# Batch 0's second feed-forward product by plain matmuls in two passes, with its weights converted in their own place

## The chip, the cores and the metric

The kernel runs on one core of one Trainium2 chip. The metric is device time in microseconds (us); a time of the kernel is the median of its runs. The five engines are named as the profile names them: PE (TensorE matmul; PEld is its weight load), DVE (VectorE), ACT (ScalarE), POOL (GpSimd) and SP (SyncE, which here only issues transfers). [...]

## The reference

Two blocks follow each other. A hash attention gives `x`; a Fourier mixing block works on it. Cut to what matters:

```python
# q, k, v: (4 batches, 8 heads, 768, 64) float32; buckets from the signs of q@proj, k@proj
scores = where(q_bucket == k_bucket, scale * q @ k.T, -1e9)
x = softmax(scores) @ v                      # (4, 768, 512)
u = x + real(fft(fft(x, axis=1), axis=2))
un = (u - mean(u)) / sqrt(var(u) + 1e-6)     # per row
out = u + relu(un @ w_ch1) @ w_ch2           # (512, 2048) and (2048, 512)
```

The two weights arrive as 64-bit floats, so the kernel has to turn them into float32 itself. The change concerns the second product, `relu(...) @ w_ch2`, for the first of the four batches, and the way in which both weights come in.

## The kernel before

**Batches and stages.** The kernel goes through four batches. The attention of batch b+1 (24 steps, two heads at a time) is interleaved with the mixing of batch b. The mixing generator `mix(b)` yields after small pieces, and the main loop takes pieces from it in proportion to the attention's steps. The last batch's mixing has no attention beside it. In the first attention PE, DVE, ACT and POOL keep the written order; after it a scheduler places the instructions of every engine from the written order and its own estimates.

**The mixing** has these stages: folds and the two Fourier products (L1062, L1091), a transposition of `x` into six row tiles `u` (`across`, L1117), then for each of two halves of the 2048 hidden columns the first feed-forward product (`inner`, L1373 to L1421) and the second (`outer7`, L1221). Batch 0 therefore runs four such stages: first inner, first outer, second inner, second outer.

**Seven products for eight.** Both feed-forward products use a Strassen-like scheme (Winograd's): each matrix is cut into quarters, seven products of quarters replace eight, and sums of quarters are needed on both sides. In `outer7` a product is four matmuls of 128 x 128 weights against 256 columns, summed in one PSUM tile; three pairs of row tiles, seven products each, make 84 matmuls a half. The sums on the left side are DVE additions (`tile_sums` L1231 and L1232, L1266, L1274). The results are put together by ACT copies (L1265, L1276, L1279) and DVE additions (L1258, L1292, L1294, L1298). PSUM tiles of this stage come from a pool of two (`ps`, L521) while attention runs.

**The right side.** `right7` is seven tiles of 512 KB laid over `w2`: the quarters B11, B21, B22 and the sums T4, T1, T2, T3 for one half. For batch 0 the generator `weights2` (L1189) makes them: a row block of `w_ch2` (128 x 512, 64-bit, 512 KB) is fetched by POOL into one of two raw buffers (`zraw2`), `convert` writes its two column halves into two tiles of `right7`, and after every second block four DVE subtractions (L1212 to L1215) make the sums. Eight blocks make a half. Each half is stored to DRAM (`bd`, L1217), from where later batches fetch it (L1251). As the second half is written into the same seven tiles, its conversion can't begin before the first outer stage has read them; it runs during the second inner stage.

**A conversion** (`narrow`, L620) is DVE L631, L635 and an addition (L641 for one piece, L644 twice for two), ACT L639, L646 and L647. Only after L647 is the raw buffer free for the next fetch. The first weights (`weights1`, L703) go the same way, 16 blocks over seven raw buffers; the first seven fetches are issued by SP, the other nine by POOL (L685).

**The scratch tile `tq`** has six slots of 128 x 256. In batch 0 its first four hold the sums of quarters of the first weights for the inner stage (`quarters`, L1157, DVE L1164 to L1167, stored by SP L1170), one set for each of the eight hidden blocks; in an outer stage its slots are `temps`, for partial results.

**SP's queue** carries, in one order, the loads of q, k and v (L556, L562, L570), the stores of quarters (`ad`, L1169, L1170; `bd`, L1217), the ring of first-weight quarters for later batches (L1339) and the fetches of `right7` (L1251). POOL issues the output stores of batches 0 to 2 (L1000).

Of the kernel before, what the change touches and what calls it, by code (L numbers as in the profile page):

```python
# [20 lines left out]
P = 128  # L21
B, H, S, D = 4, 8, 768, 64
NBITS = 6
DM = H * D
# [455 lines left out]
def _main(  # L480
# [139 lines left out]
    def narrow(dst, raw, col, low=None):  # L620


        lo, hi = (raw[..., i] for i in range(2))
# [16 lines left out]
        if len(di.shape) == 2:  # L640
            nc.vector.tensor_tensor(di, di, low, op=ALU.add)  # L641
        else:
            for i in range(di.shape[1]):
                nc.vector.tensor_tensor(di[:, i], di[:, i], low[:, i], op=ALU.add)  # L644
# [27 lines left out]
    class Arrival:  # L672


        def __init__(self, slices, raws, col):
            self.slices, self.raws, self.col = slices, raws, col
            self.wide = slices[0][1].dtype == I64
            self.depth = len(raws) if self.wide else 4

        def fetch(self, i, queue):  # L680
            if i < len(self.slices):
                dst, src = self.slices[i]
                if self.wide:
                    raw = self.raws[i % self.depth].bitcast(I32)
                    queue.dma_start(raw.bitcast(I64), src)  # L685
                else:
                    n = dst.shape[-1]
                    queue.dma_start(
                        dst, src if len(dst.shape) == 2 else src.rearrange("p (s n) -> p s n", n=n)
                    )  # L690

        def convert(self, i, low=None):
            if self.wide:
                dst = self.slices[i][0]
                raw = self.raws[i % self.depth].bitcast(I32)
                if len(dst.shape) == 2:
                    raw = raw.rearrange("p (n w) -> p n w", w=2)
                else:
                    raw = raw.rearrange("p (s n w) -> p s n w", w=2, n=dst.shape[-1])
                narrow(dst, raw, self.col + i, low)  # L700
            self.fetch(i + self.depth, nc.gpsimd)

    def weights1():  # L703
# [10 lines left out]
        arrival = Arrival(slices, raws, 0)  # L714
        for i in range(arrival.depth):
            arrival.fetch(i, nc.sync)
# [472 lines left out]
    def weights2():  # L1189

        slices = []
        for half in range(2):
            for r in range(HF // 2):
                for hi, first in ((0, B11), (1, B21)):
                    c = half * HF // 2 + r + hi * HF

                    step = 1 if hi else T1 - B11
                    dst = w2f[:, 0 : 7 * QB].rearrange("p (i r n) -> p i r n", i=7, n=HD)
                    slices.append(
                        (dst[:, first : first + step + 1 : step, r],  # L1200
                         moe_w_ch2[c * P : (c + 1) * P, :])
                    )
        arrival = Arrival(slices, [zt2[:, i] for i in range(2)], NDC * DFF // WC)
        for half in range(2):
            for i in range(arrival.depth) if half == 0 else ():
                arrival.fetch(i, nc.gpsimd)
            for i in range(HF):
                arrival.convert(half * HF + i)
                yield
                if i % 2:  # L1210
                    b11, b21, b22, t4, t1, t2, t3 = (q[:, i // 2] for q in right7)
                    nc.vector.tensor_tensor(t3, b22, t1, op=ALU.subtract)  # L1212
                    nc.vector.tensor_tensor(t1, t1, b11, op=ALU.subtract)
                    nc.vector.tensor_tensor(t2, b22, t1, op=ALU.subtract)
                    nc.vector.tensor_tensor(t4, b21, t2, op=ALU.subtract)  # L1215
            for i in range(7):
                nc.sync.dma_start(bd[half, i], right7[i])  # L1217
            if half == 0:
                yield
# [350 lines left out]
```

## Time and profile before

| what | value |
|---|---|
| median of 10 runs | 1106.98 us (1104.31 to 1110.42) |
| the profiled execution's own time | 1106.58 us |
| its span, first to last instruction | 1104.8 us |
| PE busy in the span | 1049.5 us (95%) |
| DVE busy | 790.3 us (72%) |
| ACT busy | 499.6 us (45%) |
| POOL busy | 63.1 us (6%) |
| batch 0: first inner stage (first to last matmul of L1366) | 195.9 to 247.1 us |
| batch 0: first outer stage (L1246) | 262.0 to 306.7 us |
| batch 0: second inner stage | 306.9 to 369.1 us |
| batch 0: second outer stage | 369.7 to 413.2 us |

Busy time is the time in which an engine has an instruction under way. Matmuls overlap each other in the pipeline, so PE's busy time is a union, and a single matmul's duration is longer than its distance to the next one. Every float32 matmul appears as two records in the trace: the 84 matmuls of an outer half are 168 records.

### The profile page before, as it was taken

To read this page: it belongs to the slowest core of one execution; us is meant where nothing else is said; L and a number is where in the kernel's file an instruction comes from. 1 tells how busy PE (TensorE), PEld (TensorE's weight loads), DVE (VectorE), ACT (ScalarE), POOL (GpSimd) and SP (SyncE) were. 2 spreads that over 40 slices of the span, in tenths; PEclk is the share of its full clock that TensorE was granted. 3 is DMA by queue.
4 is the path that set the end of the run, shared out by engine and by line. 5 is a ranking of instruction groups with operands and counts; after the bars stand their busy time and mean duration, and the time that the engine had idled before them with its cause. 6 is when DMAs were issued, how large, how long until landed. Compare 5 with 4: busy or idle time off the path is not lost.

```text
span 1104.8 us, 14065 instructions
## 1 busy us (share of the span) xinstructions
PE 1049.5 (95%) x4893; PEld 636.5 (58%) x4893; DVE 790.3 (72%) x1326; ACT 499.6 (45%) x1055; POOL 63.1 (6%) x141
## 2 busy tenths in 40 slices
PE   6989888999999999999999999999999999999996
PEld 3333354445744675555664576645674569768675
DVE  5789968979598977786758785975856785744353
ACT  5879455654267324354425424354315532340420
POOL 0000000002000020010000011001000002100000
PEclk9999998999999999999999999999999999999998
DMA  8744434261046262323144134213032205122401
GB/s 223 202 100 106 92 106 109 93 201 26 20 126 182 79 185 60 60 60 76 26 152 107 51 67 167 43 35 94 20 109 83 68 29 172 53 82 83 127 20 42
DMA packets 175567, 103.13 MB, mean 93 GB/s; under 512 B 129408, under 2 KB 162816, under 8 KB 175488
## 3 DMA queue, kind: packets, MB, share of 16 engines
q1 hardware_dynamic: 168400, 83.93, 28.6%
q0 software_dynamic: 5520, 17.83, 5.2%
q8 instruction: 41, 0.67, 0.2%
q10 hardware_dynamic: 1568, 0.39, 0.2%
q14 instruction: 38, 0.31, 0.1%
HBM read 81.14 MB, written 20.97 MB: 92 GB/s over the span
## 4 chain that ended last, share of the span: by engine, by line
PE 56%; DVE 8%; ACT 3%; issue 1%; DMA 1%; DVEq 0%; ACTq 0%
PE o L1246 20%; PE h_p L1366 19%; PE oo L890 6%; PE sc L869 5%; PE cs L1062 2%; DVE pk L879 2%; PE A L1091 2%; PE B L1091 1%; DVE acc L964 1%; ACT rr L924 1%; DMA zraw<-in_moe_w_ch_dram 1%; DVE w L1258 1%; PE un L1117 1%; PE bits L804 1%; DVE h L1232 1%
## 5 line engine op out<-in xcount | busy, mean ns | idle before, releaser
L1246 PE MATMUL o<-w,h 128*128 128x256 f32 x1152 | 259.4, 382 | 1.1 <-ACT tq L1265 0.7
L1246 PEld LDWEIGHTS o<-w,h 128*128 128x128 f32 x1152 | 216.3, 190 | 43.5 <-issue 4.6
L873 ACT ACTIVATE pk<-sc 128x768 f32<-128x768 f32 x192 | 147.9, 809 | 82.8 <-PE sc L869 64.1
L1366 PE MATMUL h_p<-x,w 128*128 128x384 f32 x448 | 163.1, 494 | 3.8 <-ACT h L1388 2.3
L890 PE MATMUL oo<-pk,vn 128*64 128x385 f32 (+1 forms) x768 | 157.7, 505 | 3.6 <-DVE pk L879 3.0
L869 PE MATMUL sc<-qt,kt 64*128 64x384 f32 x768 | 153.8, 503 | 3.9 <-ACT pk L873 3.6
L879 DVE SCALAR_TENSOR_TENSOR pk<-qb,kb,pk 128x768 f32<-128x768 bf16 x132 | 129.1, 1013 | 29.8 <-ACT pk L873 29.6
L1366 PEld LDWEIGHTS h_p<-x,w 128*128 128x128 f32 x448 | 82.0, 190 | 71.1 <-ACT pk L873 5.4
L964 DVE TENSOR_TENSOR acc<-acc,pk 128x1536 f32<-128x1536 f32 (+1 forms) x72 | 105.8, 1483 | 6.6 <-ACT pk L873 6.1
L1366 PE MATMUL h_p<-w 128*128 128x384 f32 x288 | 105.5, 489 | 2.2 <-ACT w L1403 2.2
L890 PEld LDWEIGHTS oo<-pk,vn 128*64 128x64 f32 x768 | 49.9, 137 | 98.3 <-issue 71.0
L869 PEld LDWEIGHTS sc<-qt,kt 64*128 64x128 f32 x768 | 66.4, 186 | 48.9 <-issue 24.3
L1366 PEld LDWEIGHTS h_p<-w 128*128 128x128 f32 x288 | 53.7, 190 | 41.7 <-ACT w L1403 3.5
L1276 ACT COPY tq<-o 128x256 f32<-128x256 f32 x24 | 8.9, 372 | 105.8 <-PE o L1246 105.8
L1258 DVE SCALAR_TENSOR_TENSOR w<-o,rs,w 128x256 f32<-128x256 f32 x56 | 26.8, 479 | 41.6 <-PE o L1246 41.6
L1246 PE MATMUL o<-w 128*128 128x256 f32 x176 | 42.3, 383 | 1.4 <-DVE w L1258 1.3
L1392 DVE TENSOR_TENSOR h<-h 128x384 f32<-128x384 f32 x32 | 17.8, 556 | 32.0 <-ACT h L1391 32.0
L1265 ACT COPY tq<-o 128x256 f32<-128x256 f32 x24 | 8.9, 371 | 69.3 <-PE o L1246 69.3
L1000 POOL DMA_DIRECT2D out_dram<-w x30 | 16.3, 546 | 388.7 <-issue 293.2
L1246 PEld LDWEIGHTS o<-w 128*128 128x128 f32 x176 | 32.8, 190 | 8.8 <-DVE w L1258 2.9
L1399 DVE TENSOR_TENSOR h<-h 128x384 f32<-128x384 f32 x32 | 17.7, 553 | 26.8 <-ACT h L1398 26.8
L1292 DVE TENSOR_TENSOR tq<-tq,o 128x256 f32<-128x256 f32 x24 | 10.0, 418 | 34.7 <-PE o L1246 34.7
(170 smaller groups left out, 1350.5 us busy)
## 6 DMA issues: line engine op xcount, KB each, us to landing
w<-ad SPq DMA_DIRECT2D x168, 128.0 KB, 2.0
w<-bd SPq DMA_DIRECT2D x42, 512.0 KB, 4.4
zraw<-in_moe_w_ch_dram POOLq DMA_DIRECT2D x21, 512.0 KB, 4.2
bd<-w SPq DMA_DIRECT2D x14, 512.0 KB, 4.0
vn<-in_v_dram SPq DMA_DIRECT2D x32, 192.0 KB, 3.4
qn<-in_q_dram SPq DMA_DIRECT2D x120, 48.0 KB, 2.4
kn<-in_k_dram SPq DMA_DIRECT2D x60, 96.0 KB, 3.3
ad<-tq SPq DMA_DIRECT2D x8, 512.0 KB, 3.0
```

Source lines behind the costliest of these rows:

```text
L869: last[0] = nc.tensor.matmul(ps[:, h, 0:HALF], kt[rows, ks], qt[rows, qs], start=kb is not None, stop=True,)
L873: nc.scalar.activation(pk[:, g, :, 0:HALF], ps[:, :, 0:HALF], AF.Exp, scale=SCALE)
L879: nc.vector.scalar_tensor_tensor(w, qb[:, h].rearrange("p (g s) -> p g s", g=2), kb[:, h, c : c + 1], w, op0=ALU.is_equal, op1=ALU.mult,)
L890: nc.tensor.matmul(oos[g][h * D : (h + 1) * D, 0:w], nat["v", n][:, (2 * c + h) * D : (2 * c + h + 1) * D], pk[:, g, h, 0:w], start=(c == ...
L964: nc.vector.tensor_tensor(acc[:, g], (first if c == 1 else acc)[:, g], new[:, g], op=ALU.add,)
L1062: nc.tensor.matmul(ps[:, pc + 2 * lo : pc + 2 * hi - 1 : 2], z[:, cp, pc, par, t * P : (t + 1) * P], ch[:, cp, pc, lo:hi], start=(cp == 0) ...
L1091: nc.tensor.matmul(ps[:, cols], F[:, par, k, t, j * P : (j + 1) * P], sq[:, t, k, cols], start=(t == 0), stop=(t == 1),)
L1246: nc.tensor.matmul(ps, a[:, r], right7[i][:, r], start=start and r == 0, stop=r == HF // 2 - 1, skip_group_check=not start,)
L1258: nc.vector.scalar_tensor_tensor(t[:, cols], src, r, t[:, cols], op0=ALU.mult, op1=ALU.add)
L1366: nc.tensor.matmul(ps, left[:, k], right[i][:, k], start=start and k == 0, stop=k == 1, skip_group_check=not start,)
L1392: nc.vector.tensor_tensor(c21, c12, c21, op=ALU.add)
L1399: nc.vector.tensor_tensor(c22, c21, c22, op=ALU.add)
```

## The change

It touches four things.

- **Batch 0's outer stage** is a new function `outer` in place of `outer7`: for each of six row tiles T, in the order 3, 0, 1, 2, 4, 5, eight matmuls of 128 x 128 against all 512 columns of `w2`, summed in one PSUM tile, and one DVE operation that scales and adds the result to `u`. The two passes are the two halves of the hidden columns, as before. Batches 1 to 3 keep `outer7`.
- **`weights2`** converts each row block into its own place in `w2`, whole, in the same order of blocks. Nothing is laid over it in batch 0. The sums of quarters are no longer made there.
- **`quarters2(half)`** runs beside the outer stage: it stores the three quarters from `w2` and makes the four sums of each of four row blocks in `tq`, which one transfer stores to `bd`. Batch 1 fetches all of `right7` for its first half at the start of its `mlp7`.
- **`Arrival`** gets one queue for all its fetches: SP for the first weights, POOL for the second. Some scratch places move (`ut`, `sd`), since `w2` is now full.

```diff
         nc.scalar.activation(low, lo.bitcast(U32), AF.Copy, scale=2.0**-29)
-        if len(di.shape) == 2:
-            nc.vector.tensor_tensor(di, di, low, op=ALU.add)
-        else:
-            for i in range(di.shape[1]):
-                nc.vector.tensor_tensor(di[:, i], di[:, i], low[:, i], op=ALU.add)
+        nc.vector.tensor_tensor(di, di, low, op=ALU.add)
...
-            self.fetch(i + self.depth, nc.gpsimd)
+            self.fetch(i + self.depth)
...
-        arrival = Arrival(slices, raws, 0)
+        arrival = Arrival(slices, raws, 0, nc.sync)
...
     def weights2():
...
+        rows = [
+            half * HF // 2 + r + hi * HF
+            for half in range(2) for r in range(HF // 2) for hi in range(2)
+        ]
+        arrival = Arrival(
+            [(w2[:, c, :], moe_w_ch2[c * P : (c + 1) * P, :]) for c in rows],
+            [zt2[:, i] for i in range(2)], NDC * DFF // WC, nc.gpsimd,
+        )
+        for i in range(arrival.depth):
+            arrival.fetch(i)
+        for i in range(len(rows)):
+            arrival.convert(i)
+            yield
+
+    def quarters2(half):
+
+        lo, hi = (slice(i + half * HF // 2, i + (half + 1) * HF // 2) for i in (0, HF))
+        for i, rows, n in ((B11, lo, 0), (B21, hi, 0), (B22, hi, HD)):
+            nc.sync.dma_start(bd[half, i], w2[:, rows, n : n + HD])
+        t4, t1, t2, t3 = (tq[:, i] for i in range(4))
+        for r in range(HF // 2):
+            (b11, b12), (b21, b22) = (
+                [w2[:, i + half * HF // 2 + r, n : n + HD] for n in (0, HD)]
+                for i in (0, HF)
+            )
+            nc.vector.tensor_tensor(t1, b12, b11, op=ALU.subtract)
+            nc.vector.tensor_tensor(t2, b22, t1, op=ALU.subtract)
+            nc.vector.tensor_tensor(t4, b21, t2, op=ALU.subtract)
+            nc.vector.tensor_tensor(t3, b22, b12, op=ALU.subtract)
+            nc.sync.dma_start(
+                bd[half, T4:, :, r].rearrange("i p n -> p i n"), tq[:, 0:4]
+            )
+            yield
+
+    def outer(b, half, hall, ut, rs):
+
+        quarters = quarters2(half)
+        for T in (3, 0, 1, 2, 4, 5):
+            u = ut[T]
             if half == 0:
-                yield
+                rs[T] = spread(b, T, u)
+            ps = pt([P, DM], f"o{b}_{half}_{T}")
+            for i in range(2):
+                for r in range(HF // 2):
+                    nc.tensor.matmul(
+                        ps, hall[:, i, r, T * P : (T + 1) * P],
+                        w2[:, half * HF // 2 + r + i * HF, :],
+                        start=(i + r == 0), stop=(i == 1 and r == HF // 2 - 1),
+                    )
+                if i == 0:
+                    next(quarters, None)
+                    yield
+            nc.vector.scalar_tensor_tensor(u, ps, rs[T], u, op0=ALU.mult, op1=ALU.add)
+            if half:
+                store(b, T, u, slice(0, DM))
+            yield
...
-                if j == GT - 1 and (b < B - 1 if half else b > 0):
+                if j == GT - 1 and (b < B - 1 or half == 0):
                     nc.sync.dma_start(right7[i], bd[1 - half, i])
...
-        ut, sd, ss = [*us], side, s1s
+        ut, sd = [*us], side
+        if b == 1:
+            for i in range(7):
+                nc.sync.dma_start(right7[i], bd[0, i])
...
-            yield from outer7(b, half, hall, ut, rs, ss)
+            yield from (outer7 if b else outer)(b, half, hall, ut, rs)
...
-            other = after(2 + NT, other, islice(arrival2, HF + 1))
+            other = after(2 + NT, other, islice(arrival2, HF))
```

## The prediction

> **What bounds the kernel now.** I read the page first, then the table of windows cut at batch 0's stages, then the tiles and lines that the change touches, then the waits.
>
> The page: PE is busy in nearly every slice once batch 0's mixing runs, DVE often nearly as much.
>
> ```profile
> PE 1049.5 (95%) x4893; PEld 636.5 (58%) x4893; DVE 790.3 (72%) x1326; ACT 499.6 (45%) x1055; POOL 63.1 (6%) x141
> PE   6989888999999999999999999999999999999996
> DVE  5789968979598977786758785975856785744353
> ```
>
> Busy PE isn't PE at its peak, so I go to stages. The windows (length, then each engine's busy time and instructions) are, in order: batch 0's first inner stage, the passage to the outer stage, first outer, second inner, second outer, and the second inner stage of batches 1 and 2.
>
> ```profile
> 195.90:247.40 51.50, 48.24 (x164) 23.97 (x162) 41.73 (x76) 28.53 (x58) 2.11 (x4) 1.00 0.48 158
> 247.40:262.00 14.60, 12.52 (x69) 5.05 (x68) 12.35 (x21) 9.29 (x23) 1.53 (x4) 1.00 0.26 48
> 262.00:306.90 44.90, 44.55 (x219) 34.53 (x219) 32.07 (x55) 11.54 (x22) 6.07 (x9) 1.00 0.04 13
> 306.90:369.70 62.80, 58.62 (x236) 27.68 (x235) 58.47 (x113) 43.65 (x93) 2.64 (x5) 1.00 0.56 166
> 369.70:413.60 43.90, 42.85 (x206) 33.19 (x202) 36.34 (x75) 9.56 (x26) 6.92 (x13) 1.00 0.42 118
> 571.00:629.70 58.70, 57.83 (x239) 28.16 (x235) 44.37 (x67) 32.34 (x68) 0.00 (x0) 1.00 0.34 86
> 830.50:886.90 56.40, 56.35 (x224) 27.88 (x222) 41.47 (x63) 30.89 (x64) 0.00 (x0) 1.00 0.23 68
> ```
>
> To see: in both outer stages PE works all but 0.35 and 1.05 us, while DVE has 13 and 8 us to spare. There PE alone sets the time. In the second inner stage DVE is at 93%, PE idles 4.2 us, and the stage is 4.1 us longer than the same work in batch 1, 6.4 longer than in batch 2. The conversions are what batch 0 has on top. In the passage DVE is at 85% and PE idles 2.1 us of 14.6.
>
> What a matmul costs by its columns (durations minimum/median/maximum in ns; 256 columns in the outer stage, 512 in the averages of the first weights):
>
> ```profile
> L1246 PE MATMUL o<-w,h x1152: 379/379/483, 262.0 to 1095.2; 128*128 128x256 f32 x192
> L656 PE MATMUL ws<-w,ones x32: 590/592/617, 38.2 to 126.0; 128*32 128x512 f32 x32
>   ACT tq L1265: 69.3, 18
> ```
>
> 256 more columns take 592 - 379 = 213 ns more, 0.83 ns a column. The last line, under "who waited for it", shows ACT waiting for PE, not the reverse.
>
> **What the Trainium skill says.** (1) "Perfetto Trace Analysis", section "Identifying the Most-Contended Engine": matmul busy share is no good measure of how near PE is to its limit. The trace agrees: start to start, two outer records lie 216 ns apart at the median, though each shows 379. (2) "FP8 and Floating Point Precision", "TensorE Precision Notes": true FP32 takes four passes through the array. Two records a matmul at 213 ns for 256 columns agree, if a record is two passes at 2.4 columns a ns. (3) "VectorE: DVE Perf Modes", "The TRN2 errata": a float32 tensor_tensor takes (N+151)/0.96 ns. L1231 with 512 columns shows 689 against 691, L1212 with 256 shows 420 against 424. (4) "DMA: Bandwidth & Descriptors", "Issuing engines are not separate DMA queues": another issuer saves only its own time to issue. Nothing in the trace speaks against it: a 512 KB fetch of zraw lands after 4.2 us from POOL when nothing else is under way.
>
> **The change part by part.**
>
> *1. The products.* Removed: 84 matmuls, 168 records a half, at 216 ns: 36.3 us. Added: 6 x 8 = 48 matmuls, 96 records, at 216 + 213 = 429 ns: 41.2 us. That is +4.9 a half, the eight products for seven. The additions on the left and the copies go, and with them small waits of PE: before these products DVE and ACT ended 15 us of its idle time over the eight halves (L1246's list "sat idle until"), 1.9 a half, a part of it the attention's; I take 0.5 off. **+4.4 a half, +8.8 in all**, with PE as the bound. Bounds +3.5 and +5 a half.
>
> *2. DVE and ACT beside them.* Removed for each of three pairs: L1231, L1232, L1266, L1274 (4 x 0.69), six L1258 (0.48), three of L1292 to L1298 (0.42): 6.9 us, 20.7 a half; ACT 9 copies of 0.37. Added: six operations on 512 columns from PSUM at 481 + 267 = 748 ns (256 more columns at 0.96 a ns): 4.5 us, and 16 subtractions at 0.42: 6.7 us. DVE is 9.5 us lighter a half. Worth **nothing**: PE's unbroken work hides all of it already. Without that cover it would be a gain.
>
> *3. The conversions.* Those of the second half needn't wait for the first outer stage any more. In the order of the built program four of the eight now stand in the first inner stage, three in and around the passage, one beside the first outer stage. The second inner stage loses 8 x (0.42 + 0.69 + 2 x 0.42) = 15.6 us of DVE, 16 subtractions (6.7), and 8 x 2.33 = 18.6 of ACT. What that is worth is read from batch 1's same stage: **-4.1**; bounds -2 (batch 0 keeps its own `quarters`) and -6.4 (batch 2).
>
> *4. What they press on.* First inner stage and passage take seven conversions (13.7 us of DVE, 16 of ACT) and the sums of two row blocks (3.4), and lose those of three (5.0) and L1231 and L1232 of two pairs (2.8): DVE +9.3. The inner stage has 10 us of free DVE for its +3. The passage gets +6 and has 2.2 free; its PE waits on DVE's masks and ACT's row scales. About 2 of the 6 stand behind the last mask, where nothing of the passage waits for them, so 4 less some overlap: I take **+3.5**; bounds -1 (the sums that go were in the way too) and +8 (a fetch of 4.2 us is waited for as well; before L631 DVE has such waits of 1.2 and 1.5 us).
>
> *5. The sums' scratch.* `tq` is single: the first subtraction of a row block waits until the 512 KB of the block before have landed (a store to `bd` takes 4.0 us), and behind it in DVE's order stand the attention's masks and the L1258-like operation that frees one of two PSUM tiles. Each tile is 16 records, 6.9 us of PE, so PE stops only when DVE is more than 6.9 us late. In both halves that operation of the second tile stands behind three landings, near the edge. I take **+0.75 a half, +1.5**; bounds 0 and +3 a half.
>
> *6. First weights by SP.* Nine fetches of 0.5 us to issue leave POOL and stand in SP's order among the loads of q, k, v. A fetch waits for a conversion, and the loads behind it too: the third pair's k load moves behind a fetch that can't issue before 69.6 us (end of the ninth L647), from about 60 to 71. Its buffer is refilled for the fifth pair only at 111 us, so some 30 us of slack hide it. POOL has nothing else then. **0**; bounds -2 and +2; without the slack it would be up to 10.
>
> *7. Queue and reload.* `bd` is stored by 7 issues a half instead of 7, and batch 1's seven reloads of 512 KB stand on SP behind the end of the first outer stage (four) and the second (three). Their first reader is at 516 us, 100 us later. The output stores are fewer (POOL). **0**; bounds 0 and +1.
>
> Sum: 8.8 - 4.1 + 3.5 + 1.5 = **+9.7 us**. The profiled execution took 1106.58 (1104.8 of span and 1.8 around it), so 1116.3; it stands 0.4 below the median of the ten runs, which would give 1116.7. I say **1116.3**.
>
> **The rivals.**
>
> *Faster: DVE was the bound around the outer stages.* If the freed 19 us of DVE shorten what follows (second inner stage down to batch 2's 56.4, -6.4; first inner and passage -3 as the sums leave; outer stages +3.5 each; first stage -1), it is 7 - 10.4 = -3.4: 1103. For it: DVE at 93% in the second inner stage. Against: the outer stages themselves, where PE has no idle time to give, lengthen by arithmetic. It decides when the inner stages and the passage together give more than 9 us. Chance 0.10.
>
> *Level:* same, with +4 a half and 8 us given back: 0.10.
>
> *Jam:* raw buffers and `tq` both make DVE wait for landings; the passage and first inner stage +8, the outer stages +3 each on top: 8.8 - 4.1 + 8 + 6 = +18.7, 1125. For it: POOL's fetches waited 105 us for L647. Against: the order spreads the conversions over 60 us. Chance 0.17.
>
> *It doesn't do what it says:* the scheduler could have left the second half's conversions where they were; their place in the order excludes it. The forecast itself has 0.63.
>
> **How the numbers follow.** About 0.2%, 2.2 us, can be told from no change. Slower: 0.63 + 0.17 = 0.80; same 0.10; faster 0.10. The range: with part 1 at its middle, parts 3 and 4 at their lower bounds and no wait for `tq`, it is 8.8 - 6.4 - 1 = +1.4, 1108; the level case reaches down to 1104.5, and **1105** takes in most of it. Upward **1124** takes in most of the jam.
>
> **What would show it.** In the profile after: 192 records of 512 columns for batch 0, about 430 ns apart; first outer stage 49 to 50 us long, second 48 to 49; second inner stage near 58 with DVE under 45; passage and first inner 69 to 70 together; L1258-like operations waiting for PE and PE not for them. The prediction is wrong if the outer stages grow by less than 3 us each, or if the first 190 us move by more than 2.

## The result, and the profile after

The kernel after takes 1109.62 us (median of 9 runs, 1107.67 to 1111.78), the kernel before beside it 1106.39 us (31 runs). The ratio is 1.0030 with a 95% interval of 1.0017 to 1.0043, or +3.2 us. Three later comparisons of the same two kernels gave 1.0060, 1.0043 and 1.0061, so the mean of four is 1.0049, about +5.4 us. The forecast was +9.7 us: the direction and the range (1105 to 1124) hold, but the size was too large, three times the first comparison and 1.8 times the mean of four. The difference between these four is not explained: the stages below account for the mean, not for the +3.2.

The profiled execution of the kernel after took 1113.3 us, its span 1111.5. First the lines of its page that answer to those shown of before (the last is the granted TensorE clock):

```profile
PE 1059.2 (95%) x4749; PEld 609.9 (55%) x4749; DVE 762.7 (69%) x1244; ACT 493.0 (44%) x1037; POOL 53.9 (5%) x124
...
PE   7989897889999999999999999999999999999996
...
DVE  5889968878366855885857786875866875644353
...
PEclk9999999998999999999999999999999999999999
```

DVE lost 27.6 us of work and PE gained 9.7, yet such sums don't say where the time went. The windows do, cut at the same places of batch 0 and of batches 1 and 2 as before (length, then PE, PEld, DVE, ACT and POOL busy with instructions, the clock, the DMA share, GB/s):

```profile
193.00:247.40 54.40, 47.72 (x163) 23.01 (x162) 43.52 (x74) 33.61 (x71) 4.84 (x9) 1.00 0.45 136
247.40:264.90 17.50, 14.91 (x71) 5.62 (x69) 16.43 (x31) 15.09 (x36) 2.35 (x5) 0.88 0.68 172
264.90:315.20 50.30, 50.30 (x147) 21.38 (x147) 23.93 (x39) 7.23 (x12) 4.08 (x7) 0.97 0.25 85
315.20:374.10 58.90, 58.24 (x231) 27.69 (x230) 41.59 (x64) 31.67 (x66) 0.00 (x0) 1.00 0.34 87
374.10:421.10 47.00, 47.00 (x135) 19.93 (x134) 29.32 (x60) 7.18 (x19) 3.89 (x7) 1.00 0.46 121
578.30:636.80 58.50, 57.63 (x236) 28.13 (x234) 44.16 (x67) 32.38 (x68) 0.00 (x0) 1.00 0.34 84
837.70:894.00 56.30, 56.25 (x224) 27.84 (x222) 41.38 (x63) 30.91 (x64) 0.00 (x0) 1.00 0.22 67
```

In both outer stages PE's busy time equals the length of the window: PE never stops. The second inner stage is 58.9 us with DVE at 41.6, like batch 1's. The first inner stage and the passage are longer than before (51.5 and 14.6), with DVE at 94% in the passage, and there and at the start of the first outer stage the granted clock is below 1 (0.88 and 0.97): half of it was granted from 260.8 to 267.7 us. Batches 1 and 2 have not moved.

One execution is not enough for a few us, so the stages are set side by side from two profiles of the kernel before and four of the kernel after. "Two stages" are the first inner stage and the passage; the second outer stage runs to the next Fourier matmul; "rest" is what follows.

| us | before (two profiles) | after (four profiles) | mean change |
|---|---|---|---|
| start of the first inner stage | 195.9, 194.8 | 193.0, 192.2, 195.2, 192.9 | -2.0 |
| two stages | 66.1, 65.8 | 71.9, 72.0, 68.6, 70.5 | +4.8 |
| first outer | 44.9, 44.9 | 50.5, 49.5, 49.1, 49.1 | +4.7 |
| second inner | 62.7, 63.2 | 58.9, 58.9, 58.9, 58.9 | -4.0 |
| second outer | 45.4, 45.4 | 48.4, 48.4, 48.4, 48.4 | +3.0 |
| rest | 689.8, 690.0 | 688.8, 689.1, 689.0, 689.1 | -0.9 |

The sum is about +5.5, close to the mean of the four comparisons. The second outer stage has the same length in all executions, the first outer stage nearly so, the stages ahead of them have not.

### The profile page after: what moved, and what is told of

Its sections match the earlier page's. It is cut to its first block, busy times and chain, and to the rows that moved or that the text cites. A ratio compares the mean times of both kernels' runs of the same rounds, so it can differ in the third digit from the quotient of the medians.

```text
span 1111.5 us, 13613 instructions
## 1 busy us (share of the span) xinstructions
PE 1059.2 (95%) x4749; PEld 609.9 (55%) x4749; DVE 762.7 (69%) x1244; ACT 493.0 (44%) x1037; POOL 53.9 (5%) x124
## 4 chain that ended last, share of the span: by engine, by line
PE 68%; DVE 10%; ACT 4%; DMA 3%; issue 2%; SPq 0%; POOL 0%; DVEq 0%; ACTq 0%
PE h_p L1383 21%; PE o L1261 18%; PE oo L878 8%; PE o L1223 8%; PE sc L857 7%; DMA zraw<-in_moe_w_ch_dram 2%; PE cs L1050 2%; DVE pk L867 2%; PE A L1079 2%; DVE acc L952 1%; PE B L1079 1%; ACT rr L912 1%; PE bits L792 1%; PE un L1105 1%; DMA kn<-in_k_dram 1%
## 5 line engine op out<-in xcount | busy, mean ns | idle before, releaser
L1261 PE MATMUL o<-w,h 128*128 128x256 f32 x864 | 194.0, 381 | 0.1
L1261 PEld LDWEIGHTS o<-w,h 128*128 128x128 f32 x864 | 162.4, 190 | 31.5 <-issue 3.2
L878 PE MATMUL oo<-pk,vn 128*64 128x385 f32 (+1 forms) x768 | 155.4, 503 | 2.3 <-DVE pk L867 1.8
L1383 PEld LDWEIGHTS h_p<-x,w 128*128 128x128 f32 x448 | 81.7, 190 | 70.5 <-ACT pk L861 6.0
L1223 PE MATMUL o<-w,h 128*128 128x512 f32 x192 | 85.6, 604 | 0.0
L1223 PEld LDWEIGHTS o<-w,h 128*128 128x128 f32 x192 | 36.4, 193 | 46.8 <-issue 43.5
L1291 ACT COPY tq<-o 128x256 f32<-128x256 f32 x18 | 6.7, 373 | 80.6 <-PE o L1261 80.6
L1273 DVE SCALAR_TENSOR_TENSOR w<-o,rs,w 128x256 f32<-128x256 f32 x42 | 20.0, 479 | 29.8 <-PE o L1261 29.7
L1261 PE MATMUL o<-w 128*128 128x256 f32 x144 | 34.7, 384 | 1.4 <-DVE w L1273 1.3
L1050 PE MATMUL cs<-ch,z 128*128 128x128 f32 (+3 forms) x192 | 32.3, 318 | 2.3 <-DVE bt L796 1.3
L1050 PEld LDWEIGHTS cs<-ch,z 128*128 128x128 f32 x192 | 27.1, 191 | 11.3 <-issue 3.9
```

The source lines that it names most:

```text
L878: nc.tensor.matmul(oos[g][h * D : (h + 1) * D, 0:w], nat["v", n][:, (2 * c + h) * D : (2 * c + h + 1) * D], pk[:, g, h, 0:w], start=(c == ...
L1050: nc.tensor.matmul(ps[:, pc + 2 * lo : pc + 2 * hi - 1 : 2], z[:, cp, pc, par, t * P : (t + 1) * P], ch[:, cp, pc, lo:hi], start=(cp == 0) ...
L1223: nc.tensor.matmul(ps, hall[:, i, r, T * P : (T + 1) * P], w2[:, half * HF // 2 + r + i * HF, :], start=(i + r == 0), stop=(i == 1 and r = ...
L1261: nc.tensor.matmul(ps, a[:, r], right7[i][:, r], start=start and r == 0, stop=r == HF // 2 - 1, skip_group_check=not start,)
L1273: nc.vector.scalar_tensor_tensor(t[:, cols], src, r, t[:, cols], op0=ALU.mult, op1=ALU.add)
L1383: nc.tensor.matmul(ps, left[:, k], right[i][:, k], start=start and k == 0, stop=k == 1, skip_group_check=not start,)
```

## The experiments

A ratio is always against the kernel before, timed beside it on the same chip. A landing is the moment at which a transfer's data have arrived. The freeing operation is the DVE operation that reads an outer tile out of PSUM, so that its buffer can take another tile.

### Who fetches the first weights

The kernel before with the later fetches by SP, the kernel after with them by POOL, and the kernel after as it is:

```diff
 # e1_before_sp, e14_before_sp_again: in convert() of the kernel before
-self.fetch(i + self.depth, nc.gpsimd)
+self.fetch(i + self.depth, nc.gpsimd if self.col else nc.sync)
 # e2_after_pool, e15_after_pool_again: in fetch() of the kernel after
-self.queue.dma_start(raw.bitcast(I64), src)
+(nc.gpsimd if i >= 7 else self.queue).dma_start(raw.bitcast(I64), src)
```

> The kernel before with one thing of the change: all fetches of the first weights issued by SP. The order on PE, DVE and ACT is the same as before, only nine fetches move from POOL to SP. Theory A (in the profile after, the first 45 us are 3.1 us shorter because POOL's early refetch no longer competes with the third block's fetch, for which ACT and DVE waited until 25.7 us): about 3 us faster than before, 1103.3, and the lead stands complete at 45 us. Rival (my prediction's step 6: the queue is worth nothing, and the 3.1 us are one execution's accident, such as the half clock granted at 30 us in the profile before): within 1 us of before.

> The changed kernel with that one thing undone: the nine later fetches of the first weights issued by POOL again, order on PE, DVE and ACT as in the changed kernel. Theory A: 3 us slower than the changed kernel, so 6 us slower than before (1.0057). Rival: as the changed kernel, 3 us slower than before (1.003).

> The changed kernel unchanged, for a second profile. The first profiled execution took 1113.3 us, 3.7 more than the median of its runs, and was granted half the clock from 260.8 to 267.7 us, in the passage and the start of the first outer stage. Theory: that half clock is particular to the execution; with it absent the first outer stage is 47 to 48 us instead of 50.3 and the execution near 1109.6. Rival: the half clock comes in every execution at this place, and the stage is 50 again.

Measured: 0.9999 (0.9985 to 1.0012) for SP in the kernel before; 1.0063 (1.0038 to 1.0088) with POOL and 1.0060 (1.0039 to 1.0081) with SP in the kernel after. Timed, the issuer is worth nothing that can be told. The traces said otherwise: the start of the first inner stage came at 191.3 us in e1_before_sp as against 195.9. So both were repeated, with the kernel before against itself:

> The kernel before, unchanged, timed against itself. Theory (the first profile of it had a long start by chance of the half-clock stretches): the first inner stage begins near 193 us, as in the kernel before with SP's fetches (191.3), ratio 1.000. Rival (fetches by POOL make the start 2 to 4 us longer): it begins at 195 to 197 us again.

> The kernel before with the first weights' later fetches by SP, a second time. Theory (fetches by SP are worth nothing that can be told): ratio 0.9990 to 1.0010 with an interval that holds 1, and the first inner stage begins within 1.5 us of the run before it. Rival (they are worth 2 to 3 us): ratio 0.997 to 0.998 and a beginning 2 to 4 us earlier.

> The kernel after with the first weights' later fetches by POOL as in the kernel before, a second time. Theory (worth nothing): the kernel after's ratio, 1.003 to 1.006, within 0.1% of the next run. Rival (worth 2 to 3 us): 0.2 to 0.3% above the next run.

> The kernel after, unchanged, beside the run before it. Theory: ratio 1.0040 to 1.0060; first inner stage and passage 68.6 us without a half-clock stretch in them and 72 with 6.8 us of it. Rival: as in the first result, 1.003 or less.

Measured: 0.9989 (0.9974 to 1.0005), 1.0004 (0.9991 to 1.0016), 1.0063 (1.0042 to 1.0084) and 1.0061 (1.0041 to 1.0081). SP or POOL, the times agree to 0.05%. The expectation of e3_after_again missed: half clock came again at 261.6 us, and the first outer stage took 49.5 us. The start came at 194.8 us (before), 195.3 (before, SP), 196.4 (after, POOL) and 192.9 (after, SP). In the kernel after SP does bring the first inner stage some 3 us forward (four starts from 192.2 to 195.2 against 196.4 twice), but the two stages then take 68.6 to 72.0 us where with POOL they took 68.6 and 68.1: the first outer stage begins at 263.4 to 264.9 with SP and at 265.0 and 264.4 with POOL. Part of this is the clock: in both executions with POOL, and in the SP one that starts at 195.2, a stretch of 6.8 us of half clock ends within 2 us of the first inner stage's start; in the other three with SP the last of it falls later, in the two stages and at the start of the first outer one. In the kernel before, the traces show no such return (the first outer stage begins at 257.1 and 260.2 us with SP, at 262.0 and 260.6 with POOL); there only the timing speaks for nothing gained.

### Whether PE alone sets the outer stages

One of the eight matmuls of each outer tile is left out:

```diff
-for r in range(HF // 2):
+for r in range(HF // 2 - i):
     nc.tensor.matmul(
 ...
-    start=(i + r == 0), stop=(i == 1 and r == HF // 2 - 1),
+    start=(i + r == 0), stop=(i == 1 and r == HF // 2 - 2),
```

> The changed kernel with one of the eight matmuls of each row tile left out in batch 0's outer stages (the last row block of each half is not multiplied), so that PE has as many columns to go through as the seven products had. Order otherwise as in the changed kernel. If PE alone sets the outer stages (the prediction's step 1): 12 records of 429 ns less a half, 5.15 us, 10.3 in all, so 1099.3, 0.9936 of before, with both outer stages 5.1 shorter. Rival (DVE, the landings of tq or the masks hold the outer stages): less than 5 us in all, and PE waits for the operation that frees its PSUM tile.

Measured: 0.9957 (0.9934 to 0.9979), 1099.09 us, against 1111.57 of the kernel after on that chip. The windows of its two outer stages, in the same columns:

```profile
261.40:305.30 43.90, 43.90 (x135) 18.53 (x135) 25.31 (x42) 8.29 (x13) 4.37 (x8) 1.00 0.28 94
364.20:405.60 41.40, 41.40 (x122) 17.52 (x116) 29.13 (x60) 7.18 (x19) 3.89 (x7) 1.00 0.49 128
```

Twelve records at 429 ns are 5.15 us. The stages went from 49.1 to 44.0 and from 48.4 to 43.3: 5.1 each. PE is still without a gap. That the number of matmuls times their spacing sets the length of a plain outer stage is shown. (The time fell by 12.5 us, 2.3 more than this; the first inner stage and passage alone differ by up to 3.4 us between executions of the kernel after.)

### Where the conversions stand

The eight conversions of the second half stand in the first inner stage and the passage (one in the first outer stage). In two runs they were held back by writing one element into their destination: until the first outer stage begins, and until it has ended.

```diff
 # e5_beside, ahead of conversions 8 and 9; two more calls of the generator in outer()
+nc.vector.tensor_copy(w2[0:1, rows[i], 0:1], w1[0:1, 2, 0:1])
 ...
 # e6_late, at the end of the first half's outer()
+elif T == 5:
+    for i in (HF // 2, HF + HF // 2):
+        nc.vector.tensor_copy(w2[0:1, i : i + HF // 2, 0], u[0:1, 0 : HF // 2])
```

> The kernel after, with the eight second-half conversions held until the first outer stage begins; nothing is left out. Theory (the outer stages are PE's alone, and in the kernel after the conversions lengthen the first inner stage and the passage together from 66.1 to about 70 to 72 us): those two go back to 66 to 68 us; the first outer stage takes 15.6 us more of DVE and 18.6 of ACT and stays at 49 to 50 us, since DVE has about 25 us to spare there; the second inner stage stays at 58.9. In all 3 to 5 us less than the kernel after, a ratio to the kernel before of about 1.001 to 1.003. Rival (the passage is long because of the attention and the stores of the sums, not the conversions): the first inner stage and the passage stay at 69 or more, ratio 1.004 to 1.007. Second rival (DVE's order counts in the outer stage too: the operation that frees a PSUM tile stands behind conversions): first outer stage 52 us or more.

> The kernel after, with the eight second-half conversions held until the first outer stage has ended, so that they stand in the second inner stage, as in the kernel before; nothing is left out. Theory: second inner stage back to 62 to 63 us (DVE near 57), first inner stage and passage 66 to 68, first outer stage 49 to 50, second outer 48.4: against the kernel after the same within 1.5 us, and 7 to 10 us (ratio 1.006 to 1.009) over the kernel before if all the rest of the change gives nothing back. Rival (the second inner stage got shorter because the sums of the quarters left it, not the conversions): it stays at 59 to 60, and the ratio is 1.002 to 1.005.

Measured: 1.0054 (1.0035 to 1.0073) and 1.0065 (1.0046 to 1.0084). The windows of e6_late (first inner, passage, first outer, second inner):

```profile
193.80:242.90 49.10, 46.61 (x163) 23.45 (x162) 37.41 (x62) 26.68 (x55) 2.72 (x5) 1.00 0.36 108
242.90:257.20 14.30, 12.83 (x71) 5.05 (x69) 10.97 (x20) 9.48 (x24) 0.90 (x2) 1.00 0.58 136
257.20:306.30 49.10, 49.10 (x147) 20.85 (x147) 22.78 (x37) 6.27 (x9) 3.27 (x8) 1.00 0.17 55
306.30:371.00 64.70, 58.69 (x235) 27.56 (x233) 53.90 (x91) 45.20 (x96) 3.27 (x6) 1.00 0.56 152
```

Without the second half's conversions the two stages take 63.4 us, less than in the kernel before: the rest of the change gives 2.6 us back there, and the conversions cost 5.2 us (against 68.6, an execution with no half clock in these stages) to 8.6 (against 72.0, with half clock). In the second inner stage they cost 5.8 us (64.7 as against 58.9). So the rival of e6_late, that the departed sums shortened that stage, falls; its theory said 62 to 63 us. In e5_beside the two stages are 63.4 as well, but the first outer stage took 56.6 us. Its window, then a wait of PE that the kernel after has not, and DVE's waits for landings:

```profile
257.00:313.50 56.50, 52.08 (x147) 21.76 (x147) 35.98 (x63) 21.95 (x39) 11.52 (x14) 0.94 0.40 131
...
PE o L1225 <- DVE w L1235: 3.9, 1, 3.9
...
DVE w L631 <- DMA zraw<-in_moe_w_ch_dram: 8.0, 3, 4.5
```

L1235 is the freeing operation (L1231 in the kernel after). The tile whose buffer PE needed next was complete at 285.5 us. DVE, which keeps the order of the program, waited until 287.4 us for a landing, did the two conversions that stood in front, and came to the freeing operation only at 292.3. PE had 3.7 us of the attention's matmuls in between and then stopped. The conversions before had already made DVE late: the first four freeing operations came 5.2 to 6.8 us after the last matmul of their tile. Half clock from 291.7 to 298.5 us slowed PE further, by an estimated 2.7 us, half of the 5.4 us that it worked under it. The second rival of e5_beside is what happened. A free engine is no cover when the wrong instruction stands first in its order.

### What makes the conversions dear

Two more runs took away one suspected cost each: the range test of the second weights, and the sums of the quarters.

```diff
 # e7_no_check, in narrow(): L642 and L643 for the first weights only
+if col < NDC * DFF // WC:
 # e8_no_sums, in quarters2()
-for i, rows, n in ((B11, lo, 0), (B21, hi, 0), (B22, hi, HD)):
+for i, rows, n in ((B11, lo, 0), (B21, hi, 0), (B22, hi, HD),
+                   (T4, hi, 0), (T1, lo, HD), (T2, hi, HD), (T3, lo, 0)):
 ...
-for r in range(HF // 2):
+for r in range(0):
```

> The kernel after, with the range test of the second weights left out (ACT's L642 and L643 with the read of its accumulator, 691 + 774 + 191 = 1.66 us a conversion), so that a raw buffer is free 1.66 us earlier for its next fetch. Theory (in first inner stage and passage the conversions wait for raw buffers' round trips, ACT 11.3 us for landings, and ACT's row scales stand behind them): first inner stage and passage together 2 to 4 us less than in the kernel after, that is 67 to 69; second inner stage the same 58.9 as it has no conversions. Rival (DVE's own work, 43.5 of 54.4 and 16.4 of 17.5 us, is what lengthens them): less than 1.5 us of change there.

> The kernel after, without the sums of the second weights' quarters: plain quarters are stored in their place, so 32 subtractions of 0.42 us (13.4 us of DVE, about half in each half) and their use of the scratch tile are left out. Theory (PE alone sets the outer stages, the scratch's landings hold up nothing): first outer stage 49 to 50.5 and second 48.4, unchanged; the passage 1 to 2.6 us shorter, since 6.7 us of DVE leave its surroundings. Rival (the scratch tile's landings and the sums cost what the prediction took for them, 0.75 us a half): both outer stages about 0.75 us shorter, and the passage unchanged.

e7_no_check measured 1.0109 (1.0089 to 1.0128), slower than the kernel after; both expectations missed. The two stages took 74.4 us, with 10.2 us of half clock in them. With lighter conversions the order placed them differently, and ACT stood in front of late landings with the inner stage's row operations behind it. The two windows, then waits of ACT and of PE there:

```profile
194.00:254.00 60.00, 51.34 (x172) 25.52 (x170) 48.73 (x83) 27.46 (x54) 5.90 (x11) 0.93 0.47 141
254.00:268.40 14.40, 13.30 (x70) 5.24 (x68) 13.17 (x24) 8.97 (x22) 0.90 (x2) 0.95 0.58 135
...
ACT zraw L639 <- DMA zraw<-in_moe_w_ch_dram: 14.4, 7, 4.2
...
PE h_p L1383 <- ACT h L1405: 4.8, 1, 4.8
PE h_p L1383 <- ACT h L1415: 3.6, 1, 3.6
```

As two things changed, the run says nothing on the price of the range test. It shows that two late landings in the wrong place stopped PE for 4.8 and 3.6 us, and that half clock set in during the one wait and behind the other.

e8_no_sums measured 1.0062 (1.0040 to 1.0083). Its first and second outer windows:

```profile
264.70:314.00 49.30, 49.30 (x148) 20.99 (x148) 19.86 (x28) 7.27 (x12) 3.96 (x7) 1.00 0.29 98
...
372.80:419.30 46.50, 46.50 (x134) 19.80 (x128) 25.40 (x48) 7.17 (x19) 3.88 (x7) 1.00 0.36 86
```

Both are as long as with the sums, though DVE does some 4 us less in each. The scratch tile and the sums cost nothing in the outer stages. The two stages stayed at 72.8 us (with 6.6 us of half clock in them), so my theory's 1 to 2.6 us in the passage is a miss.

Then two more raw buffers, laid in rows of the second weights that are converted last:

```diff
 # e9_four_raw, in weights2()
-[zt2[:, i] for i in range(2)], NDC * DFF // WC, nc.gpsimd,
+[zt2[:, 0], zt2[:, 1]] + [w2[:, c : c + 2, :].rearrange("p c n -> p (c n)")
+    for c in (14, 6)], NDC * DFF // WC, nc.gpsimd,
 ...
```

> The kernel after with four raw buffers for the second weights instead of two (the two more lie in rows of the second weights that are converted last; from the fifteenth conversion on only the first two are used), so that a fetch has the time of three more conversions to land; nothing is left out. The eight second-half conversions still stand in first inner stage and passage. Theory (what lengthens these two stages is mostly engines standing in order behind a landing that is late: ACT waited 10 to 14 us for landings there and PE then for ACT's row operations): ACT's waits for landings under 4 us, first inner stage and passage together 66 to 69 us instead of 69 to 72. Rival (the 15.5 us of DVE and 18.6 of ACT themselves are too much for the two stages): 69 or more, though the waits for landings go.

> The kernel after, unchanged, beside the others on the same chip. Theory: 5 to 7 us over the kernel before (1.0045 to 1.0065), since the stages of its two profiles sum to 5 to 7; first inner stage and passage 69 us where no stretch of half TensorE clock falls in them and 72 where 6.8 us of it do. Rival (the first result, 1.003, was the better measure and the other chip's 1.006 is an outlier): 1.002 to 1.004.

Measured: 1.0043 (1.0030 to 1.0056) for four buffers, 1.0043 (1.0029 to 1.0057) for the kernel after beside it. ACT's largest item of waits for landings in the two stages (total, times, longest), first the kernel after, then four buffers:

```profile
ACT zraw L639 <- DMA zraw<-in_moe_w_ch_dram: 9.9, 6, 2.4
```

```profile
ACT w L639 <- DMA w<-in_moe_w_ch_dram: 2.9, 1, 2.9
```

The two windows with four buffers:

```profile
196.50:247.20 50.70, 47.03 (x156) 23.52 (x154) 42.16 (x75) 34.16 (x72) 4.95 (x8) 0.97 0.44 136
247.20:263.10 15.90, 13.48 (x71) 5.24 (x69) 13.67 (x26) 12.38 (x32) 0.90 (x2) 1.00 0.60 156
```

Most of the waits for landings went, and the two stages fell from 68.6 to 66.6 us as my theory had it; but the first inner stage began at 196.5 instead of 195.2, the first outer stage at 263.1 instead of 263.8, and the time is the same. So four buffers gain nothing in all. How the price within the two stages divides between landings and work this run does not show, for two more things moved: DVE had 55.8 us of work there instead of 58.2, as less of the attention's fell into them, and 3.4 us of half clock fell into the first inner stage. That the 15.5 us of DVE and 18.6 us of ACT are too much for these stages is an inference: no run left the conversions' work out.

### A better place, and a better half

Last, the conversions in the first outer stage again, two directly behind each of the first four freeing operations, none ahead of the first; and on top of that the seven products kept for the second half. By then the first half's weights have been read, so their place holds the sums, made in the second inner stage:

```diff
 # e10_spread, in outer() behind the freeing operation (also in e11_mixed)
+elif T < 4:
+    k = HF // 2 + (T + 1) % 4
+    nc.vector.tensor_copy(w2[0:1, k : k + HF + 1 : HF, 0], u[0:1, 0:2])
+    next(arrival2, None)
+    next(arrival2, None)
 # e11_mixed: seven views of w2, four of them over the first half's rows
+mixed = [w2[:, c : c + HF // 2, n : n + HD] for c, n in (
+    (HF // 2, 0), (HF + HF // 2, 0), (HF + HF // 2, HD),
+    (0, 0), (0, HD), (HF, 0), (HF, HD))]
 ...
-yield from (outer7 if b else outer)(b, half, hall, ut, rs)
+yield from (outer7 if b or half else outer)(b, half, hall, ut, rs)
```

> The kernel after, with the second-half conversions held back two at a time behind each of the first four outer tiles of the first half, each pair behind the operation that frees the tile's PSUM buffer, so that none stands in front of it; nothing is left out. Theory (DVE has 25 us to spare beside PE's 49 if no landing stands in front of the freeing operation): first inner stage and passage 63.4 together, as in the two runs that took the conversions out of them, first outer stage 49 to 50.5, second inner 58.9, second outer 48.4: 6 to 9 us less than the kernel after, ratio to before 0.998 to 1.001. Rival (conversions cost 5 to 8 us in any stage, because their landings stop DVE, ACT and what stands behind them): first outer stage 54 us or more, ratio 1.004 to 1.007.

> As the run before, and in the second half the seven products of quarters instead of the plain ones: the second half's sums are made in the second inner stage, one row block after each of its row blocks, in the storage of the first half's weights, which have been read by then; nothing is left out. Theory (in the second inner stage 16 subtractions of 0.42 us have 17 us of free DVE; in the outer stage 168 records at 216 ns take 36.3 us and 96 at 429 ns 41.2): second inner stage 59 to 60, second outer 45.4, so 2 to 3 us less than the run before it, and the ratio 0.996 to 0.999. Rival (the sums cost in the inner stage what they save behind it): second inner stage 61 to 62, no gain over the run before it.

> The version of e11_mixed, unchanged, a second time. Theory (its stages by the trace: 120.9 us from the end of the mixing to the first outer stage's start as against 124 to 125 in the kernel before, then 51.1 against 44.9, 59.5 against 63.1 and 44.8 against 45.4, so about -1.5 to -2 us in all): ratio 0.997 to 0.999. Rival (the first result was the edge of no difference): an interval that holds 1.

Measured: e10_spread 0.9999 (0.9986 to 1.0011), 1105.11 us: 4.8 us below the kernel after on that chip, level with the kernel before. e11_mixed 0.9981 (0.9970 to 0.9992), 1103.32 us, and a second time 0.9987 (0.9976 to 0.9997). Of the versions that leave nothing out it is the one that beats both, the kernel before by 1.6 to 2 us. (The last expectation's 120.9 us from the end of the mixing run, by the trace, from the first Fourier matmul, at 133.6 us, to 255.1 us, and are 121.5.) The first outer stage of e10_spread, then the first outer, second inner and second outer of e11_mixed:

```profile
257.00:307.50 50.50, 50.01 (x148) 21.02 (x148) 36.38 (x66) 21.42 (x39) 6.64 (x14) 1.00 0.45 147
```

```profile
255.10:306.20 51.10, 49.88 (x147) 21.03 (x147) 36.40 (x66) 21.47 (x39) 6.64 (x14) 1.00 0.37 124
306.20:365.70 59.50, 58.43 (x235) 27.78 (x233) 46.67 (x85) 31.63 (x66) 0.00 (x0) 1.00 0.36 96
365.70:408.80 43.10, 42.62 (x206) 32.94 (x202) 35.95 (x75) 10.43 (x28) 6.99 (x13) 1.00 0.36 93
```

DVE's work in the first outer stage rose from 24 to 36 us and the stage only from 49.1 to 50.5: the same conversions that cost 5 to 9 us ahead of it, and 5.8 behind it, cost 1.4 here. Waits of DVE and of PE in that stage of e10_spread:

```profile
DVE w L631 <- DMA zraw<-in_moe_w_ch_dram: 9.3, 4, 3.8
...
PE o L1223 <- DVE w L1231: 0.5, 1, 0.5
```

DVE waits for landings even longer than in e5_beside (9.3 against 8.0 us), and here too a pair of conversions stands between one freeing operation and the next. The difference is when DVE comes to them: as no conversion stands ahead of the first freeing operation, the first five come 0.0 to 3.9 us after their tile's last matmul, not 5.2 to 6.8, and a tile is 6.9 us of matmuls. For the fourth tile, behind which PE has the 3.7 us of the attention's matmuls, it is 3.4 us instead of 6.8; with the operation's own 0.75 us that gives waits of about 0.5 and 3.8 us, close to the measured 0.5 and 3.9. So a late landing costs PE only what goes beyond this cover. The rest of the 1.4 us is not explained. The second inner stage took 5 us of subtractions more for 0.6 us of length, and the second outer stage fell from 48.4 to 44.8.

## Why the prediction was right and wrong

| term of the sum (us) | forecast | by the stages |
|---|---|---|
| 1 and 5, first outer stage | +5.15 | +4.7 (4.2 in two of four profiles) |
| 1 and 5, second outer stage | +5.15 | +3.0 |
| 3, second inner stage | -4.1 | -4.0 |
| 4 and 6, to the start of the first outer stage | +3.5 | +2.8 |
| 7 and what follows | 0 | -0.9 |

**1, the products: right mechanism, one term too small.** The row of the outer matmuls in the kernel after (durations minimum/median/maximum in ns):

```profile
L1223 PE MATMUL o<-w,h x192: 592/592/1219, 264.9 to 420.7; 128*128 128x512 f32 x192
```

There are 192 records of the duration that the row of the averages had shown, 429 ns apart at the median as worked out, and PE sets the stages; 1219 is a record at half clock. What failed is "I take 0.5 off": in the second half the seven-product stage had more slack than that. From the trace, the distances from the start of an outer matmul to the next start on PE sum to 37.2 us in the first half of the kernel before and 38.7 in the second, for 168 x 216 = 36.3; the second half contains one distance of 1.13 and one of 0.67 us, at waits for an ACT copy and for a row operation. In the kernel after they sum to 41.9 (in executions without half clock there) and 41.8, for 96 x 429 = 41.2. So the products cost +4.7 and +3.1, 7.8 in all and not 8.8. The 15 us from which I took the 0.5 were misread as well: that list adds the idle time of the weight loads (PEld) to PE's. For the matmuls alone the list is

```profile
  DVE w L1258: 1.3, 3
  ACT tq L1265: 0.7, 1
  ACT h L1417: 0.3, 1
```

which is 2.3 us over the eight halves, and the 0.7 and 0.3 both fall into batch 0's second outer stage. So an average, even of the right list, could not give that stage's slack. My own mark of "less than 3 us each" was only just cleared by the second stage.

**5, the scratch: wrong, worth nothing.** DVE's waits in the second outer stage of the kernel after:

```profile
DVE u L1231 <- PE o L1223: 6.1, 1, 6.1
DVE w L1231 <- PE o L1223: 1.9, 2, 1.4
DVE tq L1204 <- DMA bd<-tq: 1.9, 2, 0.9
```

The landings do make DVE wait, twice, 0.9 us each; but the freeing operations still arrive in time, and three of them themselves wait for PE. The step that failed is "near the edge": the margin of 6.9 us was never used up. (It is too wide for the fourth tile, where e5_beside and e10_spread show 3.7 us.) e8_no_sums shows the same. These 1.5 us and the 1.0 of term 1 are 2.5 of the 4.2 us by which the forecast lies above the sum of the stages; the first inner stage and passage with what lies ahead (0.7) and the end of the kernel (0.9) are nearly all of the rest. The first comparison, +3.2, lies another 2.3 us lower, and for that no stage is found.

**2, DVE's relief: right** as a gain of nothing, and it had a use that I didn't see: with the right order the first outer stage takes the conversions at 1.4 us (e10_spread).

**3, the second inner stage: right**, to 0.1 us, from batch 1's same stage; e6_late shows that it is the conversions.

**4 and 6: the sum nearly right, the parts not.** The two stages cost +4.8 where I had +3.5, with conversions at 5 to 9 and 2.6 given back by what left. The working was wrong in its count: I added seven conversions, but by DVE's first operation of each (L631) the two stages hold nine where they held four, as fewer of the first half's stand there. DVE's work rose from 54.1 to 60.0 us (58.2 in e12_after_again), not by 9.3, and yet the stages lengthened by more than the +3.5: the arithmetic of free DVE time does not price them. ACT's work rose from 37.8 to 48.7 us, and the working gave it no price of its own. In e9_four_raw fewer waits for landings gained nothing in all; what does bound these stages stays open. The 2 us by which the first inner stage starts earlier offset part of the +4.8. "The first 190 us move by more than 2" was met in three of the four profiles, but as the timed pairs agree to 0.05%, term 6 stands at 0. What I had not priced is the clock: stretches of half clock in the two stages and just behind them (6.8 us of it in the first profile) lengthen that execution by up to 3.4 us, half their length, and of the four executions the one with none in the two stages had 68.6, the one with 3.4 us 70.5.

**7: right, as far as the queues go.** (The 4.2 us of a fetch, which I read as those of an idle queue, are the median of POOL's 21 fetches, 3.6 to 9.3 us under whatever else was moving.) The 0.9 us after the second outer stage were not pursued; their cause stays open.

**The rivals.** The faster one needed more than 9 us from the stages around; the second inner stage gave 4.0, what follows 0.9, and what lies ahead took 2.8. The jam did not happen: PE never waits in the outer stages. But e5_beside shows PE stopped there by late landings, with conversions in that stage. The level case, "+4 a half and 8 us given back", came nearer in its outer stages than the forecast did, though not in what was given back.

Between single comparisons the size stays uncertain: 1.0030 and 1.0061 have intervals that barely touch (1.0043 and 1.0041).

## What to carry to other kernels

Where one engine sets a stage, a change of its instructions can be priced by start-to-start spacing from two rows, but only if the slack of the old stage is measured in that same stage and not averaged over its cousins. Work freed on another engine is worth nothing until something is moved under it, and then its place in that engine's order decides: the same conversions cost one stage 7.5 us (an estimated 2.7 of it by half clock) when they began ahead of the first operation that frees a PSUM tile, and 1.4 when they began behind it. Judge a shift of a few us by several profiles and by the point at which the next fixed stage begins.

## What the runs showed of the hardware

The half clock was the surprise. The 19 profiles of these kernels hold 42 stretches of half TensorE clock ahead of the one at the end, each 3.4, 6.8 or 10.2 us long. In every one, PE's records (their ends are modelled) cover less than half, 21 to 48%, of the 3.4 us ahead of it, without PE standing still for all of them: in e3_after_again the longest idle time in the 3.4 us ahead of the stretch at 261.6 us was 0.95 us. The changes of the clock lie on one grid of 3.41 us in each execution. Of the full-clock intervals of that grid, all 23 with PE under 42% busy were followed by half clock and none above 48.5%; of the 38 between, half were. The Trainium skill, "TensorE: Matmul & The Clock Gate", section "What's actually happening", puts the half clock after at least one idle window of about 3.4 us; the trace agrees on the length and shows that no full window of idleness is needed: under 42% busy was enough each time. So short waits close together can cost a second time, and as the grid lies differently in each execution, the same kernel shows the stretches at different places.
